# Attention with polynomial sketches and a squared-ReLU FFN on one core: five edits at the start, one at the end

## The chip, the core and the metric

The kernel runs on one NeuronCore of a Trainium2 chip. The metric is the device time of one execution in microseconds; before the change the median of three runs is 184.01 us (183.97 to 184.29). A profiled execution gives the trace from which the lines below come. The engines are TensorE (PE; its weight loads are PEld), VectorE (DVE), ScalarE (ACT), GpSimd (POOL), and SyncE (SP), which issues the DMAs.

## The reference

Batch 4, heads 4, sequence 1088, head dimension 32, sketch width 8, d_model 128, d_ff 2048:

```python
def phi(x):
    a = np.einsum('rd,bhsd->bhsr', S1, x)
    b = np.einsum('rd,bhsd->bhsr', S2, x)
    return np.einsum('bhsi,bhsj->bhsij', a, b).reshape(*x.shape[:-1], r * r)
q_p, k_p = phi(q), phi(k)
kv  = np.einsum('bhsf,bhsd->bhfd', k_p, v)
z   = np.sum(k_p, axis=2)
num = np.einsum('bhsf,bhfd->bhsd', q_p, kv)
den = np.einsum('bhsf,bhf->bhs', q_p, z)[..., None] + 1e-06
x   = (num / den) -> 4352 rows of 128        # heads side by side
out = np.maximum(x @ w_in, 0) ** 2 @ w_out
```

## The kernel before

**Stages.** Every query needs the sums `kv` and `z` of its whole batch, and every FFN row needs all four heads. The FFN is the bulk of the work: the 4352 rows are cut into ten chunks `FC` of 256 to 512 rows, and each chunk passes through 16 blocks of 128 hidden columns. One or two blocks together make a *unit*: `ffn1` (L600) multiplies by w_in into a PSUM tile `pg`, `relu` (L612, or L610 on VectorE) and `square` (L623 on ScalarE, L625 on VectorE) make `g`, and `ffn2` (L644) adds the block's share to the chunk's PSUM tile `po`. The second layer is in fp32 and takes two passes per matmul; the first is in fp32r and takes one. `f_oT` (L648) and `f_out` (L658) transpose and store a finished chunk; `f_last` (L666) stores the last one, whose two halves of 128 rows lie in two PSUM tiles, `po` and `pol`.

**The first 256 rows** are written out by hand (L702 to L857), for they stand before everything: k arrives and is transposed, `a_kf` (L313) multiplies four tiles of k by both sketches into PSUM tiles `kf`, ScalarE copies the second factor into `kb`, `a_kp0` (L331) multiplies the factors into `kp`, and `a_kv0` (L396) sums kp times v, and kp times ones, over nine tiles of 128 rows into the PSUM tile `kvp`. Meanwhile `q0` (L754) makes the queries' features. From `kvp` VectorE takes `zb`, `bd` and `zm`; then come the denominators `den0` (they begin with a matmul of `eps`, L790), the numerators `num0`, the reciprocals, and `xT`, the FFN's input.

**The chunks of attention after that** (batch 0 from row 256 on in two chunks, then each batch at a time) go through `q_tasks` and `nd_tasks`. `a_qc` sketches the queries on TensorE, `a_qt` to `a_rc` make the reciprocals of the denominators on VectorE (`rc`), `a_rl` (L508) places them by 16 small GpSimd copies into `rd`, `a_qs` and `a_qp` make the features, `a_nd` (L543) multiplies them by `kv` (64 small passes), `a_bc` (L559) spreads `rd` over the columns, and `a_x` multiplies into `xT`. The first of these chunks is called (0, 8): batch 0, rows 256 to 639.

**Order.** `tc.manual_schedule()` keeps every engine's instructions in the order in which they are written. Beyond the part by hand, `_Order` writes it: it plays the operations through with a cost for each engine, a key (a due time), the operations that each needs, and the number of buffers in each ring, and emits them by their planned start. The FFN's matmuls have a fixed sequence among themselves. An instruction waits by semaphores for what it really needs, and all that stands behind it on its engine waits too.

**PSUM rings.** `psf` has two tags, `pg` and `po`, of two tiles each, taken in turn. In the part by hand `pg` goes to a warm-up tile, `kf` of the second and fourth group, `kvp`, `num0`; `po` goes to `sp`, `kf` of the first and third group, `den0`, a warm-up tile. `kvp` takes the place of the second group's `kf`, and so waits until the second `kp` has read it.

**Loads.** All are issued by SP in one queue, and each waits until the one eight issues before it has landed. For batch 0: k, q's first 256 columns of each partition's row, v in eight pieces (L199), q's next 384; then the weights in quarters: w_in 0, 1, 2, w_o 0, 1, w_in 3, w_o 2, 3, then the rest of q. GpSimd casts each quarter of w_in to fp32r (`cast_wi`, L688) when it has landed. Quarter c serves the hidden blocks 4c to 4c + 3. Then the loads of batch 1 (k, four of v, q) and batch 2 stand in the queue.

Of the kernel before, what the change touches and what calls it, by code (L numbers as in the profile page):

```python
# [107 lines left out]
def kernel(  # L108
# [20 lines left out]
    LU = 4  # L129
    KC = [(0, 160), (160, 128)]  # L130
    W0, W1, W3 = 8, 0, 1
    ND, QT, WI, KL, QL = 2, 6.0, (1.0, 1.9), (30.0, 8.0), 4.0

# [24 lines left out]
    def sb(name, cols, dt=F32, rows=128):  # L160
        return cpool.tile([rows, cols], dt, tag=name, name=name)
# [80 lines left out]

    kt0 = sb("kt0", SP)
    nc.vector.memset(_ap(kt0, 0, 128, 128 * (NT - 2) + 96, [[128, 2], [1, 32]]), 0.0)
    eps = sb("eps", 192, rows=1)
    nc.vector.memset(eps[:, 0:64], 1e-6)
    nc.vector.memset(eps[:, 64:192], 1.0)
    zb = sb("zb", 130)
    nc.gpsimd.memset(zb[:, :], 0.0)
    own_p = sb("own_p", 2)  # L250
# [59 lines left out]
                )  # L310


    def a_kf(t0, n, pool, tag, w=32):  # L313
        kf = pool.tile([128, 512], F32, tag=tag, name="kf")
        for t in range(n):
            for c in range(0, 128, w):
                o = 128 * (t0 + t) + c
                nc.tensor.matmul(
                    _ap(kf, c, w, 32 * t, [[32 * n, 2], [1, 32]]),
                    kt0[:, o : o + w],  # L320
                    sf,
                )
        kb = wpool.tile([128, 32 * 3], F32, tag="kb", bufs=4, name="kb")
        nc.scalar.copy(kb[:, 0 : 32 * n], kf[:, 32 * n : 64 * n])
        st["kf", t0] = kf, kb
# [182 lines left out]
    def a_rl(b, i0, nb, c):  # L508
# [3 lines left out]
        for h in range(H):  # L512
# [2 lines left out]
                st["rc"][32 * c : 32 * c + 32, n * h : n * h + n],  # L515
            )

    def a_qs(b, i0, nb, which, x):
        m = 8 * nb
        if x == 0:  # L520
            st[b, which, i0] = wpool.tile([128, 4 * 32 * NT], F32, tag=which, bufs=1, name=which)
        nc.vector.stream_shuffle(  # L522
            in_=banks(st[b, "qc", i0], 2 * x, 0, m),
            out=_ap(st[b, which, i0], 0, 128, 2 * m * x, [[m, 2], [1, m]]),
            mask=mask_b if which == "qb" else mask_a[int(which[2])],
        )
# [139 lines left out]
    def f_last(c0):  # L666
        po, b = st["po", c0], B - 1


        def store(i):  # L670
            for x, eng in enumerate((nc.sync, nc.scalar)):
                eng.dma_start(
                    bass.AP(
                        out.tensor,
                        out.offset + (b * S + 16 * x * G + (c0 - b * S) // 32 + 4 * i) * 128,
                        [[G * 128, 16], [128, 4], [1, 128]],
                    ),
                    ob[i][64 * x : 64 * x + 64, :],
                )

        ob = [fpool.tile([128, 128], F32, tag="obl", bufs=2, name="obl") for _ in range(2)]
        nc.scalar.copy(ob[0][:, :], po[0][:, 0:128])
        store(0)
        nc.vector.tensor_copy(ob[1][:, :], po[1][:, 0:128])
        store(1)

    def cast_wi(c):
# [21 lines left out]
    nc.scalar.copy(ss[:, :], sp[:, 0:80])  # L709
    load_q(nc.sync, 0, 256, 640)  # L710
    load_wi(nc.sync, 0)
    load_wi(nc.sync, 1)
    load_wi(nc.sync, 2)
    load_wo(nc.sync, 0)
    load_wo(nc.sync, 1)
    load_wi(nc.sync, 3)
    for c in range(2, 4):
        load_wo(nc.sync, c)
    load_q(nc.sync, 0, 640, S)
    keep_warm(W1)  # L720
    keep_warm(1, 384)
    a_kT0(0, 2)
    a_kT0(2, 2)
    for x in range(2):
# [41 lines left out]
    a_kp0(0, 2)  # L766
    a_kf(2, 2, psf, "pg")
    a_kf(4, 3, psf, "po")
    a_kf(7, 2, psf, "pg", 64)
    q0(0)  # L770
    q0(1)
    for i in range(2):
# [1 line left out]
            _ap(qb0, 64 * i, 64, 0, [[256, 2], [1, 256]]),  # L774
            _ap(x0, 64 - 64 * i, 64, 0, [[512, 2], [1, 256]]),
        )
    st[0, "kvp"] = psf.tile([128, 512], F32, tag="pg", name="kvp")
    for t0, n in ((0, 2), (2, 2), (4, 3), (7, 2)):
        if t0:
            a_kp0(t0, n)  # L780
# [5 lines left out]
        in1=_ap(qb0, 0, 128, 0, [[256, 2], [1, 256]]), op=mult,  # L786
    )
    den0 = psf.tile([128, 512], F32, tag="po", name="den0")
    for y in range(2):
        nc.tensor.matmul(  # L790
            den0[64 * y : 64 * y + 64, 0:128], eps[0:1, 0:64], eps[0:1, 64:192],
            start=True, stop=False,
        )
    bd = sb("bd", 128)
    own = _ap(own_p, 0, 128, 0, [[0, 2], [1, 2], [0, 32]])

# [26 lines left out]
    for g in range(2):  # L823
        for y in range(2):
            o = 65 * y + 1 - g
            nc.tensor.matmul(  # L826
                den0[64 * y : 64 * y + 64, 0:128], zb[:, o : o + 64],
                qp0[:, 256 * y + 128 * g : 256 * y + 128 * g + 128], start=False, stop=(g == 1),
            )
    for y in range(2):  # L830
        nc.tensor.matmul(
# [56 lines left out]
    def q_tasks(b, i0, nb, key):  # L888
# [34 lines left out]
            ("rc", b, i0), {"DVE": 0.2 + 0.65 * more + nb * 17 / 960}, k0 - 0.1, [], on(a_rc, nb),  # L923
            uses=[("pd", b, i0)], rings=[("rc", 1)],
        )
        for c in range(4):
            O.add(
                ("rl", b, i0, c), {"POOL": 0.8 + 1.25 * more}, k0 + 0.1 * c, [], on(a_rl, b, i0, nb, c),
                uses=[("rc", b, i0)], rings=[("rd", 2)] if c == 0 else [],
            )  # L930
        for w_ in ("qb", "qa0", "qa1"):
# [15 lines left out]
    def nd_tasks(b, i0, nb, key):  # L947
        m = 16 * nb
        qps = [("qp", b, i0, e, x) for e in range(E) for x in range(2)]
        kb, vb = NK.get((b, i0)), NV.get((b, i0))  # L950

        O.add(
            ("nd", b, i0), {"PE": 0.6 + 1.05 * max(nb, 14) / 36}, key - 3.5 - 4 * dve(m),
            [("kvr", b, h) for h in range(H)]
            + ([("kT", kb, 0), ("kT", kb, 18)] if kb else [])
            + ([("vn", vb), ("ks", vb, 3)] if vb else []),
            on(a_nd, b, i0, nb, (0,) if kb or vb else (0, 1)), uses=qps + [("qp", b, i0, 0, 0)], rings=[("att", 1)], lag=PEL,
        )
        if kb:
            def behind(eng):  # L960
                a_kc(kb, st[b, "nd", i0], start=False)
                a_nd(b, i0, nb, (1,))

            glued(("kc", kb), 0.65, ("nd", b, i0), behind)
        if vb:
            def behind(eng):
                a_kvs(vb, st[b, "nd", i0], 32 * NT, start=False)
                a_nd(b, i0, nb, (1,))

            glued(  # L970
                ("kvs", vb), 1.25, ("nd", b, i0), behind, [("kp", vb, h) for h in range(H)],
            )
        for x in range(2):
            O.add(
                ("bc", b, i0, x), {"DVE": dve(m)}, key - 2.5 - 4 * dve(m) + 0.1 * x, [], on(a_bc, b, i0, nb, x),
                uses=[("rl", b, i0, 2 * x), ("rl", b, i0, 2 * x + 1)],
                rings=[("bc", 1)] if x == 0 else [],
            )
            O.add(
                ("x", b, i0, x), {"DVE": dve(m)}, key - 2.0 - 4 * dve(m) + 0.1 * x, [], on(a_x, b, i0, nb, x),  # L980
                uses=[("bc", b, i0, x), ("nd", b, i0)]
                + ([("kc", kb)] if kb else []) + ([("kvs", vb)] if vb else []),
            )

    def loads(b):
        load_k(nc.sync, b)
        for p in range(4):
            load_v(nc.sync, b, p)
        load_q(nc.sync, b, 0, S)

    prev["qTuse"] = []
    KB = {(0, 20): 1, (2, 0): 3}
# [2 lines left out]
    def k_load(b, k0, s0):  # L995
# [2 lines left out]
            [("kvs", b - 2), ("qc", b - 2, AC[b - 2][-1][0])] if b > 2 else [],  # L998
            on(loads, b), at=s0,
        )  # L1000
        for x, y, t in (("ld", "kn", 6.0), ("kn", "vn", 3.0), ("vn", "qn", 3.0)):
            O.add((y, b), {"IO": t}, s0, [(x, b)], lambda eng: None)
        for i0, n in ((0, 18), (18, 16)):
            O.add(
                ("kT", b, i0), {"DVE": dve(32 * n)}, k0, [("kn", b), ("kc", b - 1)],
# [166 lines left out]
```

## Time and profile before

| | |
|---|---|
| median of 3 runs | 184.01 us (183.97 to 184.29) |
| the profiled execution | 183.99 us, span 182.1 us |
| granted TensorE clock, mean | 0.998 |
| busy in the span | PE 177.3, ACT 136.6, DVE 122.1, PEld 104.6, POOL 39.1 us |
| largest groups | second FFN layer 122.7 us, first 70.2 us (their spans overlap), ReLU on ACT 75.3 us |
| first FFN matmul | at 12.17 us |
| first `po` matmul | at 13.89 us |
| last matmul ends | at about 178.9 us |

In the lines below, a timeline row gives start and duration in us, then engine, line, operation, the tiles `out<-in`, shapes and how many instructions the row holds; in square brackets stands the engine's idle time before it and what ended it. [...]

### The profile page before, as it was taken

How to read it: one execution, taken by the hardware profiler on the slowest of the kernel's cores; microseconds unless marked ns; L12 is line 12 of the kernel's file. 1: busy time of each engine (PE TensorE's matmuls, PEld its weight loads, DVE VectorE, ACT ScalarE, POOL GpSimd, SP SyncE). 2: the span in 40 equal slices, each digit the busy share in tenths (PEclk: the TensorE clock that was granted, in tenths of full speed). 3: DMA queues.
4: the chain of work that ended last, by engine and by line, in shares of the span. 5: the costliest groups of instructions: out<-in, count | busy, mean ns of one | idle time of the engine just before them, and what ended most of it. 6: DMA issues, size and time to landing. Idle time of an engine off the chain costs nothing.

```text
span 182.1 us, 3998 instructions
## 1 busy us (share of the span) xinstructions
PE 177.3 (97%) x1530; PEld 104.6 (57%) x1530; DVE 122.1 (67%) x262; ACT 136.6 (75%) x259; POOL 39.1 (21%) x158
## 2 busy tenths in 40 slices
PE   8999999999999999999999999999999999999992
PEld 2768776656555655655555554545554555555792
DVE  5979879999999951899994335996353334333640
ACT  3449679759947886799937778995777777777980
POOL 3545318348200003470018000600000000000000
PEclk9999999999999999999999999999999999999999
DMA  5799993010029700000031200003003000300211
GB/s 174 196 274 337 246 257 96 7 29 0 0 47 243 175 0 4 4 2 0 0 54 24 34 0 5 0 0 59 0 4 58 0 0 6 51 0 0 35 26 29
DMA packets 26146, 11.26 MB, mean 62 GB/s; under 512 B 17936, under 2 KB 25104, under 8 KB 26128
## 3 DMA queue, kind: packets, MB, share of 16 engines
q1 hardware_dynamic: 25936, 10.95, 24.8%
q8 instruction: 12, 0.20, 0.4%
q10 hardware_dynamic: 192, 0.07, 0.1%
q14 instruction: 6, 0.05, 0.1%
HBM read 8.78 MB, written 2.23 MB: 60 GB/s over the span
## 4 chain that ended last, share of the span: by engine, by line
PE 93%; DMA 2%; DVE 2%; SPq 0%; issue 0%; ACT 0%; ACTq 0%
PE po L644 61%; PE pg L600 18%; PE nd L553 3%; DMA qn<-in_q_dram 2%; PE po L639 2%; PE pol L639 2%; PE qc L306 1%; PE nd L417 1%; PE kvp L399 1%; PE qc L350 1%; PE kvp L417 1%; DVE kp L334 1%; SPq L181 0%; DVE g L625 0%; PE nd L350 0%; PE den L826 0%
## 5 line engine op out<-in xcount | busy, mean ns | idle before, releaser
L644 PE MATMUL po<-g,w_o 128*128 128x512 f32 (+3 forms) x288 | 122.7, 547 | 0.2 <-DVE g L625 0.2
L612 ACT ACTIVATE gt<-pg 128x512 f32<-128x512 f32 (+3 forms) x144 | 75.3, 570 | 31.4 <-PE pg L600 30.9
L644 PEld LDWEIGHTS po<-g,w_o 128*128 128x128 f32 x288 | 53.4, 189 | 32.3 <-issue 24.6
L600 PE MATMUL pg<-xT,w_in 128*128 128x512 f32 (+3 forms) x160 | 70.2, 520 | 0.0
L623 ACT ACTIVATE g<-gt 128x512 f32<-128x512 f32 (+2 forms) x102 | 60.7, 623 | 1.6
L625 DVE TENSOR_TENSOR g<-gt 128x512 f32<-128x512 f32 (+3 forms) x43 | 30.4, 708 | 39.5 <-ACT gt L612 38.8
L600 PEld LDWEIGHTS pg<-xT,w_in 128*128 128x128 f32 x160 | 29.2, 190 | 28.3 <-ACT gt L612 11.5
L513 POOL COPY rd<-rc 32x9 f32<-32x9 f32 (+2 forms) x80 | 19.6, 246 | 25.8 <-DVE rc L505 22.6
L459 POOL COPY kv<-kvt 32x64 f32<-32x64 f32 x48 | 12.7, 265 | 44.6 <-DVE kvt L436 42.5
L522 DVE STREAM_SHUFFLE qa<-qc 128x576 f32<-128x576 f32 (+2 forms) x20 | 11.8, 648 | 0.0
L537 DVE TENSOR_TENSOR qp<-qa,qb 128x576 f32<-128x576 f32 (+2 forms) x20 | 10.8, 604 | 0.0
L485 DVE STREAM_TRANSPOSE qt<-qc 128x576 f32<-128x576 f32 (+2 forms) x10 | 5.8, 608 | 6.2 <-PE qc L350 4.5
L370 DVE TENSOR_TENSOR kp<-fs 128x576 f32<-128x576 f32 x12 | 8.7, 741 | 0.0
L648 DVE STREAM_TRANSPOSE oT<-po 128x512 f32<-128x512 f32 (+3 forms) x9 | 5.9, 654 | 2.1 <-PE po L644 2.1
L553 PE MATMUL nd<-qp,kv 32*32 32x288 f32 (+2 forms) x320 | 6.6, 354 | 0.0
L522 DVE STREAM_SHUFFLE qb<-qc 128x576 f32<-128x576 f32 (+2 forms) x10 | 6.1, 651 | 0.0
L570 DVE TENSOR_TENSOR xT<-nd,bc 128x576 fp32r<-128x576 f32 (+2 forms) x10 | 5.6, 592 | 0.5 <-PE nd L553 0.5
L299 DVE STREAM_TRANSPOSE qT<-qn 128x192 f32<-128x192 f32 (+3 forms) x11 | 5.8, 554 | 0.2 <-DMA qn<-in_q_dram 0.2
L639 PE MATMUL po<-w_o,g 128*128 128x128 f32 x32 | 5.8, 280 | 0.0
L639 PE MATMUL pol<-w_o,g 128*128 128x128 f32 x32 | 5.7, 275 | 0.0
L563 DVE STREAM_TRANSPOSE bc<-rd 128x576 f32<-128x576 f32 (+2 forms) x10 | 5.7, 598 | 0.0
L553 PEld LDWEIGHTS nd<-qp,kv 32*32 32x32 f32 x320 | 2.9, 103 | 3.6 <-issue 2.4
(106 smaller groups left out, 89.2 us busy)
## 6 DMA issues: line engine op xcount, KB each, us to landing
kn<-in_k_dram SPq DMA_DIRECT2D x3, 544.0 KB, 7.2
qn<-in_q_dram SPq DMA_DIRECT2D x3, 544.0 KB, 7.8
vn<-in_v_dram SPq DMA_DIRECT2D x9, 144.0 KB, 6.0
w_in<-in_moe_w_in_dram SPq DMA_DIRECT2D x4, 256.0 KB, 4.2
w_o<-in_moe_w_out_dram SPq DMA_DIRECT2D x4, 256.0 KB, 5.1
out_dram<-oT SPq DMA_DIRECT2D x12, 64.0 KB, 1.9
out_dram<-oT SPq DMA_DIRECT2D x8, 56.0 KB, 1.9
out_dram<-oT SPq DMA_DIRECT2D x8, 48.0 KB, 1.8
```

The source lines that it names most:

```text
L370: nc.vector.tensor_tensor(out=_ap(st[b, "kp"], 0, 128, 64 * NT * h, [[64, NT], [8, 8], [1, 8]]), in0=_ap(fs, 0, 128, o, [[32, NT], [1, 8], ...
L459: nc.gpsimd.tensor_copy(_ap(st[b, "kv"], 32 * c, 32, 64 * h, [[32, E], [1, 32]]), _ap(st["kvt"], 32 * h, 32, 0, [[64, E], [1, 32]]),)
L513: nc.gpsimd.tensor_copy(st[b, "rd", i0][32 * h : 32 * h + 32, n * c : n * c + n], st["rc"][32 * c : 32 * c + 32, n * h : n * h + n],)
L522: nc.vector.stream_shuffle(in_=banks(st[b, "qc", i0], 2 * x, 0, m), out=_ap(st[b, which, i0], 0, 128, 2 * m * x, [[m, 2], [1, m]]), mask=m ...
L537: nc.vector.tensor_tensor(out=st[b, "qp", i0, e][:, r], in0=st[b, f"qa{e}", i0][:, r], in1=st[b, "qb", i0][:, r], op=mult,)
L553: nc.tensor.matmul(nd[32 * h : 32 * h + 32, 512 * c : 512 * c + m], kv[r, o : o + 32], qp[r, m * h : m * h + m], start=(e == 0), stop=(e = ...
L600: nc.tensor.matmul(st["pg", u][:, n * i : n * i + n], w_in[:, 128 * (d0 + i) : 128 * (d0 + i) + 128], xT[:, c0 : c0 + n],)
L612: nc.scalar.activation(gt[:, 0:w], st["pg", u][:, 0:w], Relu)
L623: nc.scalar.activation(to, of, Square)
L625: nc.vector.tensor_tensor(out=to, in0=of, in1=of, op=mult)
L639: nc.tensor.matmul(po[x // 128][:, 0:128], g[:, x : x + 128], w, start=(d == 0), stop=(d == NB - 1),)
L644: nc.tensor.matmul(po[0][:, 0:n], w, g, start=(d == 0), stop=(d == NB - 1))
```

## The change

1. *Reciprocals of chunk (0, 8).* The 16 GpSimd copies are replaced by one VectorE multiply (`a_rm`, masks `rc` into four column groups) and four TensorE matmuls (`a_rp`) with the replicated identity `irep`, which write the placed reciprocals into columns 384 to 395 of the first chunk's `po` bank; `a_bc` reads them there. In the order that results, the four stand between the two matmuls of unit 3 in `po`, and the two `bc` come directly behind the features, before a transpose of q; the other transpose of q goes behind the transposes of k. TensorE waits for the second `bc` before it goes on in `po` after `nd`. The other chunks keep the copies.
2. *The sums `kvp`* take a tile of the ring `po` in place of `pg`, hence the tile of the first group's `kf`. The fourth `kf` is made by eight matmuls of 32 columns as the others are, no longer four of 64. The `eps` matmul is one of 128 columns in place of two of 64. One warm-up matmul of 384 columns becomes three of 128.
3. *Loads.* The quarters come in the order w_in 0, w_o 0, w_in 1, w_in 2, w_o 1, w_in 3, w_o 2, then the rest of q, then w_o 3.
4. *v of batch 1* is held: a VectorE memset of one column of 32 partitions, in the order behind the last feature multiply of chunk (0, 8), writes into the tile, and the load has to wait for it. SP's queue waits with it: the rest of v and q of batch 1, the loads of batch 2, and the first stores. v's four pieces are loaded last one first, in every later batch too.
5. *The last copy* out of `pol` is halved: VectorE takes columns 0 to 63, ScalarE 64 to 127. In the program that results, ScalarE's half waits for VectorE's.

```diff
-    eps = sb("eps", 192, rows=1)
+    eps = sb("eps", 256, rows=1)
...
+    def a_rm(nb):
+        st["rx"] = wpool.tile([128, 4 * nb], F32, tag="rx", bufs=1, name="rx")
+        nc.vector.tensor_tensor(
+            out=_ap(st["rx"], 0, 128, 0, [[nb, 4], [1, nb]]),
+            in0=_ap(st["rc"], 0, 128, 0, [[0, 4], [1, nb]]),
+            in1=_ap(own_h, 0, 128, 0, [[1, 4], [0, nb]]), op=mult,
+        )
+
+    def a_rp(b, i0, nb):
+        st[b, "rd", i0] = st["po", 0][0][:, 384 : 384 + nb]
+        for h in range(H):
+            nc.tensor.matmul(
+                st["po", 0][0][32 * h : 32 * h + 32, 384 : 384 + nb],
+                irep[:, 0:32],
+                _ap(st["rx"], 0, 128, nb // 4 * h, [[nb, 4], [1, nb // 4]]),
+                start=False, stop=True, skip_group_check=True,
+            )
...
-        nc.vector.tensor_copy(ob[1][:, :], po[1][:, 0:128])
+        nc.vector.tensor_copy(ob[1][:, 0:64], po[1][:, 0:64])
+        nc.scalar.copy(ob[1][:, 64:128], po[1][:, 64:128])
...
     load_wi(nc.sync, 0)
+    load_wo(nc.sync, 0)
     load_wi(nc.sync, 1)
     load_wi(nc.sync, 2)
-    load_wo(nc.sync, 0)
     load_wo(nc.sync, 1)
     load_wi(nc.sync, 3)
-    for c in range(2, 4):
-        load_wo(nc.sync, c)
+    load_wo(nc.sync, 2)
     load_q(nc.sync, 0, 640, S)
+    load_wo(nc.sync, 3)
...
-    keep_warm(1, 384)
+    keep_warm(3, 128)
...
-    a_kf(7, 2, psf, "pg", 64)
+    a_kf(7, 2, psf, "pg")
...
-    st[0, "kvp"] = psf.tile([128, 512], F32, tag="pg", name="kvp")
+    st[0, "kvp"] = psf.tile([128, 512], F32, tag="po", name="kvp")
...
-    for y in range(2):
-        nc.tensor.matmul(
-            den0[64 * y : 64 * y + 64, 0:128], eps[0:1, 0:64], eps[0:1, 64:192],
-            start=True, stop=False,
-        )
+    nc.tensor.matmul(
+        den0[:, 0:128], eps[0:1, 0:128], eps[0:1, 128:256],
+        start=True, stop=False, skip_group_check=True,
+    )
...
+        if (b, i0) == (0, 8):
+            O.add(
+                ("rm", b, i0), {"DVE": 0.13}, k0 - 0.1, [], on(a_rm, nb), uses=[("rc", b, i0)],
+            )
+            O.add(
+                ("rp", b, i0), {"PE": 0.15}, -1000.0, [], on(a_rp, b, i0, nb),
+                uses=[("rm", b, i0)], lag=RL,
+            )
+        for c in range(4 if (b, i0) != (0, 8) else 0):
...
+    def loads_vq(b):
+        for p in range(3, -1, -1):
             load_v(nc.sync, b, p)
         load_q(nc.sync, b, 0, S)
+
+    def hold_v(b):
+        nc.vector.memset(_ap(vn[b], 96, 32, 32 * (NT - 2) - 1, [[32 * NT, H], [1, 1]]), 0.0)
...
+        if b == 1:
+            O.add(
+                ("hold", b), {"DVE": 0.07}, -500.0, [("qp", 0, 8, 1, 1)], on(hold_v, b),
+            )
+            O.add(("ldv", b), {"SP": 1.0}, s0, [("hold", b), ("ld", b)], on(loads_vq, b))
```

## The prediction

> **What bounds the kernel now.** I read the busy time by stretches first, then the chain that ended last, then the timeline around the three places that the diff touches on TensorE's path: the start of the FFN, the first attention chunk (rows 256 to 639 of batch 0), and the end.
>
> ```profile
> 13.90:170.00 156.10, 156.10 (x1215) 88.42 (x1216) 107.27 (x225) 123.34 (x235) 32.92 (x129) 1.00 0.21 50
> 178.90:182.10 3.20, 0.00 (x0) 0.00 (x0) 0.28 (x1) 0.00 (x0) 0.00 (x0) 0.91 0.15 41
> ...
> PE 93%; DMA 2%; DVE 2%; SPq 0%; issue 0%; ACT 0%; ACTq 0%
> ```
>
> Columns of the first two lines: stretch, length, then busy time of PE, PEld, DVE, ACT, POOL. From 13.9 to 170 us TensorE is busy 156.10 of 156.10 us, at a granted clock of 1.00, and the chain is TensorE for 93%. So three things alone move the time: when the first second-layer matmul (`po`) starts, what is put into or taken out of TensorE's queue after it, and the 3.2 us behind the last matmul. Work on VectorE, GpSimd or a DMA queue counts only if TensorE comes to wait for it.
>
> ```profile
> 12.65 0.42 DVE L610 TENSOR_SCALAR gt<-pg 128x256 f32<-128x256 f32 x1 [0.31 <-PE pg L600]
> 12.90 0.62 POOL L688 CAST w_in<-w_in 128x512 fp32r<-128x512 f32 x1 [0.97 <-DMA w_in<-in_moe_w_in_dram]
> 12.99 0.80 DVE L625 TENSOR_TENSOR g<-gt 128x256 f32<-128x256 f32 x1
> 13.22 0.47 PE L600 MATMUL pg<-xT,w_in 128*128 128x256 f32 x2
> 13.71 0.41 DVE L625 TENSOR_TENSOR g<-gt 128x256 f32<-128x256 f32 x1
> 13.89 0.45 PE L644 MATMUL po<-g,w_o 128*128 128x256 f32 x1 [0.19 <-DVE g L625]
> ```
>
> The start: `po` waits for the first square `g`, which takes 0.80 us where its twin takes 0.41. A GpSimd cast of a quarter of w_in runs from 12.90 to 13.52, and 13.52 + 0.27 (256 columns at VectorE's rate of the longer rows, about 0.96 per ns) is 13.79, where `g` ends: `g` stood still until the cast was done. TensorE itself was ready at about 13.53.
>
> ```profile
> 18.17 0.58 PE L600 MATMUL pg<-xT,w_in 128*128 128x256 f32 x2
> 18.69 0.96 PE L553 MATMUL nd<-qp,kv 32*32 32x96 f32 x64
> 19.58 1.99 PE L644 MATMUL po<-g,w_o 128*128 128x256 f32 x8
> ...
> 10.81 0.25 PE L836 MATMUL x<-zm,s2f 128*32 128x8 f32 x8
> ```
>
> What small matmuls between full-size ones cost. The steady spacing of passes is 0.216 us for 256 fp32 columns and 0.117 for fp32r, so the `pg` before `nd` streams until 18.60. The 64 passes of `nd` start between 18.69 and 19.41. The `po` after it starts to load weights at 19.58 and its second pass follows 0.32 later instead of 0.216, so it streams from 19.68. Of 1.08 us put in, 0.72 are passes and 0.36 are the two changes of tile shape: 0.09 in, 0.27 out.
>
> ```profile
> 177.99 0.27 ACT L682 COPY obl<-po 128x128 f32<-128x128 f32 x1 [0.80 <-PE po L639]
> 178.89 0.29 DVE L684 COPY obl<-pol 128x128 f32<-128x128 f32 x1 [2.20 <-PE pol L639]
> ...
> L324 ACT COPY kb<-kf x4: 213/213/240, 5.4 to 6.3; 128x64 f32<-128x64 f32 x3, 128x96 f32<-128x96 f32 x1
> ...
> ACT kvt L819 <- DVE zm L810: 1.9, 1, 1.9
> ```
>
> The end: after the last matmul one VectorE copy, then the store. The last line is from the list of waits: ScalarE's copy of `kvp` had to wait for VectorE's last read of the same PSUM tile, though it needs nothing from it; that hop took 0.09 us (9.99 to 10.08).
>
> **The change part by part**, against the profiled execution (183.99 us: span 182.1 and 1.89 around it; the median is 184.01).
>
> *Reciprocals through TensorE.* Taken away: 16 GpSimd copies (15.74 to 20.07, about 0.2 us each), for which one `bc` on VectorE waited until 20.10. No gain on the path: the second `xT` ended at 20.87, and its matmul could stream only at 21.41 (after eight `po` passes), some 0.4 us to spare. Added: one VectorE multiply 128x48, 0.19 us (`zm` 128x32 0.18, `pw` 128x64 0.20), and four matmuls, eight passes of 12 columns, set between the two `po` matmuls of unit 3. Nearest row: `x<-zm,s2f`, the same tile shape and count, whose passes start within 0.07 us. With both shape changes: 0.07 + 0.36 = 0.44 us (rounded from 0.073 + 0.365). All of it is on the path, since TensorE has no idle time there. Bounds: 0.07 (shape changes hidden) to 0.55 (if each pass took as long as the 0.02 of a `kf` pass and the weights came out worse). I take 0.44, since `nd` sits between the same neighbours. [...]
>
> *New waits by it.* `bc` now reads the `po` bank, so VectorE waits for the `po` matmuls of unit 4, and TensorE waits for the second `bc` before unit 5. VectorE's `qp` ended at 18.345; plus 0.19, up to 0.2 where the new multiply meets the cast at 15.18, the new 0.06 memset and two `bc` (0.30 apart, 0.37 long) gives 19.5; TensorE comes there at 19.58 + 0.44 = 20.02. Nothing, with 0.5 to spare. Then `qT`, `g`, two `xT`, two `kT` and the other `qT` (0.33, 0.57, 0.72, 1.37, 0.33) end at about 22.75 at the latest, and `qc` wants them at 22.71 + 0.44 = 23.15.
>
> *kv sums in the other ring, four `kf` 32 wide, one eps matmul.* The sums may start when the first `kp` (6.42) instead of the second (7.02) is done, so near 6.55 instead of 7.07. But their fifth tile waits for batch 0's last v load: it is issued at 5.45 and lands 2.5 us later, and there the passes, 58 ns apart, show their one gap (8.00 to 8.11). The 40 passes after it end as before, and `zb` with them. Nothing; if that gap were not v, up to 0.25. The 0.22 us saved in `kf` goes into a wait. The eps matmul ends before `zb` allows the next one: 0 to 0.05, taken as 0. Three 128-column warm matmuls against one of 384 are equal.
>
> *w_o's first quarter second.* The quarters of w_in now land first, third, fourth, sixth. `po`'s weights landed at 8.48 + 5.1 = 13.6, just in time; now earlier, which alone gives nothing. Against that, w_in's second quarter, cast at 11.31 before, lands where the third did: cast 12.90 to 13.52. The third `pg` unit (13.22 before) needs it, so its weights load from 13.61, and by the spacing of before (weights 13.19, end of stream 13.53) `po` can go at 13.95; before, its first pass really streamed from 13.96. `g` is held by the cast just as before. Sum: 0. Bounds: 0.36 earlier, if that quarter lands 0.4 earlier, to 0.4 later, if it lands as much later. The q columns moved ahead of w_o's last quarter, which unit 7 needs only after 21.5: nothing.
>
> *v of batch 1 held.* SP waits for a VectorE memset behind the last `qp` (about 18.7), and queued behind it are q of batch 1, k, v and q of batch 2 and the first stores. v issued at 14.2 to 16.5 had landed by 23.1 in the trace; 4.5 us later is 27.6, and it is needed at 34.53. k of batch 2 (27.1, needed at 38.94) and the first store (35.46) keep several us. Nothing; if that cover went, the sums of batch 1 would stop TensorE by what is late.
>
> *The last copy halved.* VectorE's half: 0.225 us (between 4 columns 0.165 and 128 columns 0.290). ScalarE's half waits for VectorE's in the changed program's order, as `kvt` did; 0.09 for the hop and 0.213 (`kb`, also 128x64). 0.225 + 0.09 + 0.213 - 0.290 = +0.24. Bounds: -0.07 (side by side) to +0.3.
>
> Sum: 0.44 + 0.24 + 0 = +0.68, so 184.67 in the profiled execution and 184.7 beside the median.
>
> **The rivals.**
> 1. *w_in's second quarter lands early* (not slower). If it lands by 12.45, its cast is over when `g` starts, and `po` goes at 13.53. Then -0.36 + 0.44 + 0.24 = +0.32, 184.3, within the noise of a comparison. For it: between 10 and 11.5 us, when quarters of w_in were moving, the DMA rate was near 200 to 250 GB/s, and 300 to 340 from 12 on with w_o among them, so a w_o quarter in second place may clear the way. Against: loads land in the order of their issue and as many bytes stand ahead.
> 2. *The cast moves onto VectorE's next squares.* The third quarter, landing at 13.6, is cast from 13.65, and the second `g` (13.71) is held like the first: +0.55 for VectorE, which eats the margins at `nd` and `qc`, and with a quarter landing 0.3 late the sum is 0.44 + 0.24 + 0.4 = +1.1, 185.1. It decides once VectorE is over 0.5 us behind. [...]
> 3. *The shape changes cost nothing and the halves run side by side*: 0.07 - 0.07 + 0, 184.0, no change; together with an early landing 183.6. Against it stand `nd` and `kvt`.
>
> **How the numbers follow.** Likeliest, chance 0.47: 184.7. Rival 1: 0.23, 184.3. Rival 2: 0.18, 184.9 to 185.1. Rival 3: 0.12, 183.6 to 184.0. The range 184.1 to 185.1 leaves out most of rival 3 and a little of rival 2; the likeliest alone spans 184.5 to 184.9. A comparison here can't tell less than 0.2% (0.37 us) from no change, so faster is below 183.64, slower above 184.38. Faster: part of rival 3 and what I overlook, 0.09. Same: two thirds of rival 1 and the rest of rival 3, with some of the likeliest's lower bounds, 0.26. Slower: 0.65.
>
> **What would show it.** The cast of the second quarter at about 12.9 and `po` at 13.9 to 14.0; four `po<-rx` matmuls with 0.4 us between the `po` passes around them beyond their spacing; no wait of TensorE at `nd`, unit 5 or `qc`; ScalarE's half starting after VectorE's and the last store issued about 0.5 us after the last matmul's result instead of 0.3. It is wrong if `po` starts by 13.6, if the passes around the new matmuls are under 0.2 us further apart than usual, or if TensorE stops between 18 and 24 us.

## The result, and the profile after

The changed kernel takes 185.61 us (median of six runs, 185.4 to 186.24) beside 184.15 us for the kernel before in the same comparison (six runs, 183.97 to 184.78): ratio 1.0079, 95% interval 1.0057 to 1.0101. It is slower by 1.46 us. In a later comparison (h3 below) it took 185.39 us beside 184.25, ratio 1.0056, interval 1.0033 to 1.0079. The prediction had 184.7 us and a range to 185.1: the side was right, the size about half of what came.

The profiled executions took 183.99 us (span 182.1) before and 185.51 us (span 183.4) after. The first view is the busy time by stretches of the changed kernel (stretch, length, then busy time of PE, PEld, DVE, ACT, POOL), then its chain and one group of its page.

```profile
13.90:170.00 156.10, 155.69 (x1221) 87.96 (x1221) 106.84 (x226) 122.49 (x234) 29.53 (x114) 1.00 0.22 51
```

```profile
PE 97%; issue 0%; ACT 0%; DVE 0%; ACTq 0%
...
L571 PE MATMUL nd<-qp,kv 32*32 32x288 f32 (+2 forms) x320 | 7.0, 354 | 0.4 <-issue 0.4
```

Before, TensorE was busy for all of the 156.10 us; now it lacks 0.41 us. The group line names the place: `nd`, once, idle 0.4 us, ended by "issue", which means that the engine waited for nothing that the profile shows: no semaphore, no DMA of the program, no other engine. The waits of the kernel before have no such line for `nd` on PE. The timeline shows where it is; the last line is the same row in the kernel before:

```profile
34.52 0.50 PE L571 MATMUL nd<-qp,kv 32*32 32x128 f32 x32
...
36.22 0.47 PE L571 MATMUL nd<-qp,kv 32*32 32x128 f32 x22
37.10 0.43 PE L571 MATMUL nd<-qp,kv 32*32 32x128 f32 x10 [0.41 <-issue]
...
35.80 0.50 PE L553 MATMUL nd<-qp,kv 32*32 32x128 f32 x32
```

This is the first chunk of batch 1: a row of 32 `nd` passes, 80 passes of kv sums, a second row of 32. The second row breaks after 22 passes; the 23rd starts 0.673 us after the 22nd (36.424 and 37.097), where neighbours are 0.007 apart. In the kernel before, the row's first and last pass start 0.234 us apart (35.802, 36.036), after the change 1.033: 0.80 us, with some slower steps right behind the stop (the longest 0.077 us).

The start, the new matmuls and the end, from the timeline of the changed kernel:

```profile
12.18 0.62 POOL L707 CAST w_in<-w_in 128x512 fp32r<-128x512 f32 x1 [1.20 <-DMA w_in<-in_moe_w_in_dram]
...
13.23 1.16 DVE L643 TENSOR_TENSOR g<-gt 128x256 f32<-128x256 f32 x2
13.38 0.74 POOL L707 CAST w_in<-w_in 128x512 fp32r<-128x512 f32 x1 [0.58 <-DMA w_in<-in_moe_w_in_dram]
...
13.77 0.65 PE L662 MATMUL po<-g,w_o 128*128 128x256 f32 x2
```

```profile
16.43 0.59 PE L662 MATMUL po<-g,w_o 128*128 128x256 f32 x2
...
16.96 0.25 PE L529 MATMUL po<-rx,irep 128*32 128x12 f32 x8
```

```profile
180.04 0.22 DVE L702 COPY obl<-pol 128x64 f32<-128x64 f32 x1 [2.22 <-PE pol L657]
180.30 0.21 ACT L703 COPY obl<-pol 128x64 f32<-128x64 f32 x1 [0.88 <-DVE obl L702]
180.54 0.56 ACTq L690 DMA_DIRECT2D out_dram<-obl  x1
```

At the start, the cast of w_in's second quarter ran at 12.18 instead of the predicted 12.90 and was over before the first `g` (13.235 to 13.647, 0.41 us); but the next cast, 13.38 to 14.12, stood across the second `g` (13.567 to 14.396, 0.83 us). Around the four `rx` matmuls, from the `po` pass at 16.43 to the first `nd` pass, it is 2.670 us; between the same passes before, 2.290. At the end, ScalarE's half starts 0.034 us after the end of VectorE's, and from the last matmul pass to the store's issue it is 0.81 us instead of 0.63.

Where the 1.52 us between the two profiled executions come from, by the start times of the same passes in both traces. Starts are compared and not ends, since the rows of neighbours overlap: in the kernel before, a `po` pass of 256 columns lasts 0.38 us in its row, and the next one starts 0.216 us behind it.

| stretch | us |
|---|---|
| start, up to `po` of unit 2 (16.397, 16.432) | +0.04 |
| the `rx` matmuls (`po` of unit 4: 17.497, 17.909) | +0.38 |
| from there to the first `nd` of batch 1 (34.101, 34.523) | +0.01 |
| the broken row of `nd`, up to the next `po` (36.233, 37.454) | +0.80 |
| behind it, up to 60 us (59.327, 60.356) | -0.19 |
| 119 us of equal work up to the last pass (178.574, 179.727) | +0.12 |
| last pass to the store's issue | +0.18 |
| the store's issue to the end of the span (2.93, 2.89) | -0.04 |
| outside the span (1.85, 2.08) | +0.23 |

The +0.12 is 2.183 to 2.184 us for a unit of 512 rows instead of 2.180; e3, f5, g3 and h3 below, which have both `rp` and the stop described next, have it too; e1, with `rp` and no stop, and e2, with the stop and no `rp`, do not. No run settles why. What lies outside the span differs between executions: 1.77 to 2.35 us in the runs below, without order. The -0.19 is time made up behind the delay. From the `po` pass behind 41.6 us to the one behind 59.3 us it is 17.68 us in the kernel before and 17.53 in every run below that had lost time at 36 to 40 us, most of it at two passes near 55.4 and 55.9 us that the kernel before starts late; what they wait for is not shown.

### The profile page after: what moved, and what is told of

It is laid out like the page before. It is cut to its first block, busy times and chain, and to the rows that moved or that the text cites. A ratio compares the mean times of both kernels' runs of the same rounds, so it can differ in the third digit from the quotient of the medians.

```text
span 183.4 us, 4018 instructions
## 1 busy us (share of the span) xinstructions
PE 178.5 (97%) x1546; PEld 105.3 (57%) x1546; DVE 122.5 (67%) x264; ACT 136.8 (75%) x260; POOL 35.6 (19%) x142
## 4 chain that ended last, share of the span: by engine, by line
PE 97%; issue 0%; ACT 0%; DVE 0%; ACTq 0%
PE po L662 61%; PE pg L618 18%; PE nd L571 4%; PE warm L714 2%; PE po L657 2%; PE pol L657 2%; PE qc L306 2%; PE nd L417 1%; PE kvp L399 1%; PE kf L318 1%; PE qc L350 1%; PE kvp L417 1%; PE nd L350 0%; PE x L776 0%; PE den L844 0%
## 5 line engine op out<-in xcount | busy, mean ns | idle before, releaser
L513 POOL COPY rd<-rc 32x9 f32<-32x9 f32 (+1 forms) x64 | 15.9, 249 | 29.8 <-DVE rc L505 27.2
L581 DVE STREAM_TRANSPOSE bc<-rd 128x576 f32<-128x576 f32 (+1 forms) x8 | 4.9, 656 | 0.0
```

What stands on the lines that cost most here:

```text
L513: nc.gpsimd.tensor_copy(st[b, "rd", i0][32 * h : 32 * h + 32, n * c : n * c + n], st["rc"][32 * c : 32 * c + 32, n * h : n * h + n],)
```

## What stopped TensorE

My first theory, A: a block of TensorE's own instructions had not arrived. Besides the loads, the page of each kernel has a line for DMAs of kind "instruction" (here the changed kernel's; the kernel before has the same with 0.4%):

```profile
q8 instruction: 12, 0.20, 0.5%
```

That is twelve packets of 16 KB in a span. I counted TensorE's instructions in the order of the program, two for each pass (weights and matmul) and one for each wait of its own: 3103 before, 3135 after, 259 and 261 to a packet. The change adds 32 up to the stop: `rp` 16, the fourth `kf` in eight matmuls instead of four 16, two more warm-up matmuls 4, and one eps matmul less takes 4. The stop stands exactly ahead of the 1217th; 256 before it is the 961st, the eighth pass of the first `nd` row, and it is there that the trace has a packet. The DMA view of that stretch holds this one packet and nothing else:

```profile
DMA packets 1, 0.02 MB, mean 11 GB/s; under 512 B 0, under 2 KB 0, under 8 KB 0
...
q8 instruction: 1, 0.02, 5.2%
```

The window is 34.4 to 35.9 us; the packet starts at 34.566 and takes 1.24 us. Between the two borders lie small passes alone, which TensorE gets through in 1.86 us (34.569 to 36.43); the first instruction of the next block started 2.53 us after the packet. In the kernel before, the later border lay on a long `po` pass, 3.7 us behind the earlier one.

Rival B: the stop belongs to the place, to an operand, a bank or an engine that `nd` waits for. Then shifting the stream without touching anything there would leave it.

### The stream shifted, in both directions

```diff
-    keep_warm(W0)
+    keep_warm(24, 170)
```

The eight opening filler matmuls of 512 columns become 24 of 170: nearly the same columns, 32 more instructions. The same edit went into the changed kernel (e1) and into the kernel before (e2).

> The changed kernel with its eight opening filler matmuls of 512 columns cut into 24 of 170: the same columns in the same time, 32 TensorE instructions more ahead of everything else. Theory A (instruction blocks): the changed kernel stops for 0.67 us in the middle of a row of nd matmuls (36.424 to 37.097 us) because TensorE's instruction stream enters a new block of 256 instructions there, 2.5 us after it entered the one before, and the block has not come. 32 instructions more move both borders forward in the program, the earlier one back into the long matmuls ahead of nd, so that some 4 us lie between them: no stop, and 185.6 - 0.8 = 184.8 us. Theory B (the stop belongs to the place: an operand, a bank or another engine that nd waits for): the stop stays at the same matmul, 185.6 us.

> The kernel before with the same 24 fillers of 170 columns in place of 8 of 512, nothing else. Its TensorE stream is then as long up to nd as the changed kernel's. Theory A (instruction blocks): the same stop appears in the same row of nd matmuls of batch 1, within some four matmuls of the place that it has in the changed kernel, 0.6 to 0.8 us, and the time is 184.15 + 0.7 to 0.8 = 184.9 us. Theory B: nothing that nd waits for has changed, no stop, 184.15 us.

e1: 184.72 us beside 184.33, ratio 1.0029 (1.0007 to 1.0052). e2: 185.32 us, ratio 1.0058 (1.0033 to 1.0083). Timeline of the second row in e1:

```profile
36.62 0.50 PE L571 MATMUL nd<-qp,kv 32*32 32x128 f32 x32
```

The same row in e2, the kernel before with smaller fillers:

```profile
36.47 0.47 PE L553 MATMUL nd<-qp,kv 32*32 32x128 f32 x22
37.40 0.43 PE L553 MATMUL nd<-qp,kv 32*32 32x128 f32 x10 [0.46 <-issue]
```

In e1 the stop is gone. Both borders lie 16 passes earlier: the first among long matmuls, where the packet started at 31.32, and the second behind the sixth pass of this row, 5.3 us after that packet. So here, with the packet early, the border crossed in this row costs nothing by itself (two runs with an idle time left open stand further below). In e2 the kernel before, in which nothing else was altered, has got the stop, at the same 22nd pass, 0.73 us. Rival B has fallen. e2 was some 0.4 us slower than expected; its trace shows an added wait at the start, which comes back below.

### A smaller shift

```diff
-    keep_warm(W0)
+    keep_warm(16, 256)
```

> The changed kernel with 16 opening fillers of 256 columns in place of 8 of 512: 16 TensorE instructions more, half of what took the stop away. Theory A (instruction blocks): the earlier border now falls on the last po pass ahead of nd, about 0.45 us before its place in the changed kernel (34.11 against 34.57 us), the later one eight nd passes sooner. A block that takes 2.5 us from border to first use (34.569 to 37.097 us in the changed kernel) then leaves a stop of 0.2 to 0.4 us, eight passes earlier in the row; none if the sequencer reads ahead of the long passes. Against the run with 32 more instructions (no stop) 0 to 0.4 us. Theory C (any shift of the stream takes the stop away, whatever its size): no stop.

```profile
36.21 0.44 PE L571 MATMUL nd<-qp,kv 32*32 32x128 f32 x14
37.08 0.46 PE L571 MATMUL nd<-qp,kv 32*32 32x128 f32 x18 [0.43 <-issue]
```

185.33 us, ratio 1.0052 (1.0019 to 1.0084). The stop moved by the eight passes expected, so theory C has fallen, but it kept its size (0.70 us) instead of shrinking. By the count the earlier border is on the last `po` pass (34.096), as expected; but the packet did not start there, only at 34.446, beside the first `nd` pass (34.511). From the packet's start to the first instruction of the block it took 2.64 us. In the six runs with a stop this time is 2.53, 2.54, 2.30, 2.64, 2.37 and 2.58 us (after, e2, e3, f5, g3, h3). So the stop lasts until 2.3 to 2.6 us behind the packet's start. The packet itself was over before TensorE came to the border in all six (in the changed kernel at 35.81, the border at 36.43), and the first instruction followed 1.27 to 1.49 us after the packet's end. What fills that time no run shows; by theory A the block was not yet usable, though its packet had ended.

In the changed kernel TensorE gets through 256 instructions in 1.86 us between the two borders, against 2.3 to 2.6 us from a packet's start to the first instruction of its block; in the kernel before it takes 3.7 us between the borders, and there is no stop.

## The parts one by one

### `rp` alone, in the kernel before

```diff
-        for c in range(4):
...
+        if (b, i0) == (0, 8):
+            O.add(
+                ("rm", b, i0), {"DVE": 0.13}, k0 - 0.1, [], on(a_rm, nb), uses=[("rc", b, i0)],
+            )
+            O.add(
+                ("rp", b, i0), {"PE": 0.15}, -1000.0, [], on(a_rp, b, i0, nb),
+                uses=[("rm", b, i0)], lag=RL,
+            )
+        for c in range(4 if (b, i0) != (0, 8) else 0):
```

The functions `a_rm` and `a_rp` and the wait of `bc` for `rp` come with it, as in the change.

> The kernel before with rp alone: the reciprocals of units 2 and 3's neighbours (the group behind the first eight) go through rx and four TensorE matmuls instead of GpSimd's copies; loads, kv sums, den and last copy as before. It adds 16 instructions to TensorE's stream. Theory A (instruction blocks): rp costs 0.38 us where it stands, and its 16 instructions pull the later border of the pair from the po pass behind the nd rows of batch 1 to the thirtieth of the 32 passes of the second row, 1.9 us behind the row's start; the block comes 2.3 to 2.6 us after its packet starts, so the stop is 0.5 us at least, just ahead of the row's last two passes: 184.2 + 0.4 + 0.5 or more = 185.1 to 186. Theory B (no part of the stop is rp's): 184.2 + 0.4 = 184.6 us, no stop.

```profile
16.25 0.59 PE L662 MATMUL po<-g,w_o 128*128 128x256 f32 x2
16.78 0.25 PE L529 MATMUL po<-rx,irep 128*32 128x12 f32 x8
...
18.92 0.96 PE L571 MATMUL nd<-qp,kv 32*32 32x96 f32 x64
```

```profile
36.05 0.49 PE L571 MATMUL nd<-qp,kv 32*32 32x128 f32 x30
37.35 0.37 PE L571 MATMUL nd<-qp,kv 32*32 32x128 f32 x2 [0.81 <-issue]
```

185.52 us beside 184.22, ratio 1.0070 (1.0043 to 1.0096). From 16.254 to 18.924 it is 2.670 us, so `rp` costs 0.38 us where it stands, as in the changed kernel. And its 16 instructions alone bring the stop, ahead of the last two passes as counted beforehand. The stop is 1.07 us long, longer than in the changed kernel: the packet started only at 34.987, 0.54 us behind the earlier border (34.451). This one part gives about as much loss as the whole change, in part by a longer stop. The fourth `kf` in eight matmuls also adds 16 instructions and by the count would put the border at the same place; that was not run.

### `rp` taken out of the changed kernel

```diff
-    keep_warm(W0)
+    keep_warm(32, 128)
...
-            O.add(
-                ("rp", b, i0), {"PE": 0.15}, -1000.0, [], on(a_rp, b, i0, nb),
-                uses=[("rm", b, i0)], lag=RL,
-            )
-        for c in range(4 if (b, i0) != (0, 8) else 0):
...
+        for c in range(4):
...
-                uses=[("rl", b, i0, 2 * x), ("rl", b, i0, 2 * x + 1), ("rp", b, i0)],
+                uses=[("rl", b, i0, 2 * x), ("rl", b, i0, 2 * x + 1)],
```

> The changed kernel with the reciprocals of the units behind the first eight moved by GpSimd's copies again, as before the change (no rx, no rp), and 32 fillers of 128 columns at the start, which put the borders of the instruction blocks where they are in the run with 24 fillers. Theory: rp costs its 0.38 us on TensorE's chain and nothing hides behind it: that run's time less 0.38, so about 184.4 us, and po of unit 4 starts 0.38 us sooner against xT's end. Rival: with v held and GpSimd's copies behind a later start, bc comes too late for unit 5 and TensorE waits there: 184.8 us or more.

```profile
16.43 1.03 PE L662 MATMUL po<-g,w_o 128*128 128x256 f32 x4
...
18.72 0.96 PE L571 MATMUL nd<-qp,kv 32*32 32x96 f32 x64
```

The same stretch is 2.291 us now (16.430 to 18.721): the 0.38 us are back, and there is no stop. The second `xT`, which waits for GpSimd's copies, ends at 21.268, and the first-layer matmul behind it comes 0.16 us later than the spacing would have it; so the rival's wait exists, and it is smaller than `rp`. The profiled execution took 184.25 us, near the 184.4 expected, but the median is 185.23, ratio 1.0052 (1.0029 to 1.0075): a miss that the part itself does not explain. See the fillers below.

### The last copy

```diff
-        nc.vector.tensor_copy(ob[1][:, 0:64], po[1][:, 0:64])
-        nc.scalar.copy(ob[1][:, 64:128], po[1][:, 64:128])
+        nc.vector.tensor_copy(ob[1][:, :], po[1][:, 0:128])
```

e3 is the changed kernel with this edit; f4 is the kernel before with the reverse of it.

> The changed kernel with its last output copy whole on VectorE again. If the two halves run one behind the other (0.223 and 0.212 us with 0.034 between in the changed kernel's trace, against 0.290 for the whole), the time from the last matmul pass to the store's issue goes from 0.81 back to 0.63 us and the kernel takes 185.6 - 0.2 = 185.4 us. If the end is set by something else (the store of the other half), 185.6 us. The stop in nd is there in either case.

> The kernel before with its last output copy in two halves, VectorE and then ScalarE, and nothing else. By the traces so far the halves run one behind the other: 0.63 us from last pass to the store's issue become 0.81, so 184.3 + 0.2 = 184.5 us. If the halves ran side by side, 184.25 us.

```profile
179.15 0.23 DVE L684 COPY obl<-pol 128x64 f32<-128x64 f32 x1 [2.20 <-PE pol L639]
179.41 0.21 ACT L685 COPY obl<-pol 128x64 f32<-128x64 f32 x1 [0.89 <-DVE obl L684]
179.65 0.56 ACTq L672 DMA_DIRECT2D out_dram<-obl  x1
```

The lines are f4's. From the last pass to the store's issue: 0.63 us in e3 and 0.81 in f4, each the reverse of its base. Medians: e3 185.49 (ratio 1.0059, 1.0039 to 1.0078), f4 184.42 beside 184.20 (1.0020, 0.9999 to 1.0042). The halves cost 0.18 us at the end of the trace; the medians cannot settle so little. The stop in `nd` is there in e3, 0.52 us.

### The loads

```diff
     load_wi(nc.sync, 0)
+    load_wo(nc.sync, 0)
     load_wi(nc.sync, 1)
     load_wi(nc.sync, 2)
-    load_wo(nc.sync, 0)
...
+    load_wo(nc.sync, 2)
     load_q(nc.sync, 0, 640, S)
+    load_wo(nc.sync, 3)
```

f1 is the kernel before with the new order; g4 the kernel before with v of batch 1 held; g2 has both.

> The kernel before with the order of the weights' loads of the changed one and nothing else: w_o's first quarter second, queries ahead of w_o's last. Theory: w_o's quarter is there by 11.3 us, its gate value comes before the cast of w_in's quarter 1 instead of behind it, so that po starts 0.2 to 0.4 us sooner after the first pg pass, of which the second gate value, held by the next cast, gives back 0.1 to 0.2: 0 to 0.2 us faster, 184.1 to 184.3 beside before at 184.3. Rival: the gain is lost in later quarters and it is the same from unit 2 on. No stop in nd in either case.

> The kernel before with v of batch 1 held by VectorE's zero and nothing else. Theory: k of batch 1 lands about 1 us earlier, v of batch 1 later, neither ends a wait of TensorE: the same, 184.2 us, and kT of batch 1 is done 0.5 to 1 us sooner. Rival: v of batch 1, behind the hold, ends a wait of the kv sums at 34.5 us: 184.4 us or more. No stop in nd.

> The kernel before with the changed order of the weights' loads and the held v of batch 1 together. With the order alone po started 0.34 us sooner after the first pg pass and lost it again by 25 us, where k of batch 1 landed 1 us later than in before and qc of unit 6 waited for kT. Theory: the hold brings that landing back below 21 us, the gain after the losses of the second gate value (0.1 to 0.2 us) stays: 184.05 us beside 184.2. Rival: the second gate value eats it all: 184.2 us. No stop in nd.

f1: 184.37 us beside 184.20, ratio 1.0007 (0.9989 to 1.0026). g4: 184.19 beside 184.22, 1.0007 (0.9980 to 1.0034). g2: 184.45 beside 184.22, 1.0026 (1.0000 to 1.0052). None is faster. In f1 `po` started 1.38 us after the first `pg` instead of 1.72, and `nd` came 6.32 us after it instead of 6.51. My expectation for g2 took this for a gain by the new order, but it is none: f4, g3 and g4, which keep the old order, have 1.37 as well, and f4 and g4 6.32. In these the cast that held the first `g` in the profile of the kernel before (12.90) ran at 12.53, 12.30 and 12.00 and was over in time. In g4:

```profile
12.00 0.62 POOL L688 CAST w_in<-w_in 128x512 fp32r<-128x512 f32 x1 [0.24 <-DMA w_in<-in_moe_w_in_dram]
...
13.04 0.75 DVE L625 TENSOR_TENSOR g<-gt 128x256 f32<-128x256 f32 x2
...
13.58 0.65 PE L644 MATMUL po<-g,w_o 128*128 128x256 f32 x2
```

So the held `g` of the kernel before belongs to that one execution, and not to its order of loads.

Behind `nd`, f1 lost time: GpSimd's copies came later (the second `bc` at 20.50 instead of 20.10), the second `xT` ended at 21.27 instead of 20.87, and the first-layer matmul behind it left 0.20 us later than in the kernel before (21.419 and 21.222). My expectation for g2 laid this loss on k of batch 1, which landed at 21.79 instead of 20.84; f1's trace shows no wait of TensorE for it. Only in f2, in the next section, did k land later still (22.21) and stop TensorE. With the hold alone k landed at 19.66 as expected, in g2 at 21.11, not below 21 as expected, and nothing waited for it. In g2's profiled execution the quarters landed so that `po` started at 14.3.

### Without the three costs

> The kernel before with three parts of the change: the order of the weights' loads, the kv sums in the po ring, and one eps matmul of 128 columns in place of two of 64; GpSimd's reciprocals, the loads of batch 1 and the whole last copy stay. Theory (rp, the halved copy and the stop in nd are what made the change slow): no slower than before, 0 to 0.3 us faster, 184.0 to 184.3 us. Rival (the kv sums' place or the eps matmul delays the start, where the changed kernel's xT ended 0.24 us later): 184.5 us.

> The changed kernel without its three costs: the reciprocals by GpSimd's copies, the last copy whole, and 32 opening fillers of 128 columns that keep the borders of the instruction blocks out of the nd rows of batch 1; the loads, the kv sums in the po ring, the held v and the eps matmul of the change stay. Theory: from the first pg pass to the third nd row as with GpSimd's reciprocals and fillers (21.78 us, before: 21.93), and 0.63 us from last pass to the store's issue: 184.0 to 184.2 us, no slower than before. Rival (a cost that is none of the three): 184.5 us or more.

f2 (the kernel before with the new order of loads, kv sums in the `po` ring, and one eps matmul): 184.46 beside 184.20, 1.0020 (1.0000 to 1.0039). From the row of `qc` at 22.520 to `po` at 25.614 it lost 0.64 us on the kernel before, since k landed at 22.21 and kT came late; the view of the tile kT has this line among those that waited for it:

```profile
PEld qc L350: 0.8, 2
```

That is the rival's side, by another mechanism, and with an interval that begins at no change.

g1 (the changed kernel with GpSimd's copies, a whole last copy, 32 fillers of 128 columns): 184.83 beside 184.22, 1.0045 (1.0016 to 1.0073), again its rival's side. But g1's list of waits for TensorE at the start has a line that the first profiles of the kernel before and of the changed kernel lack:

```profile
PE kvp L399 <- DMA vn<-in_v_dram: 1.0, 1, 1.0
```

e2, which has fillers too, has the same line with 0.8. More instructions at the opening bring the stream's first border forward in the program. In these two the first block's packet started at 6.65 and 6.63 us instead of 8.01 in the kernel before, in the middle of v's loads, and v's last piece landed at 8.81 and 8.84 us instead of 7.97. Theory D says that this costs g1 its time; rival E, that a kept part of the change does. The last runs tell them apart: h2 has the same parts as g1 without added fillers (its opening is that of the kernel before), h3 is the changed kernel again.

```diff
-    keep_warm(32, 128)
+    keep_warm(W0)
...
-    keep_warm(3, 128)
+    keep_warm(1, 384)
...
-    a_kf(7, 2, psf, "pg")
+    a_kf(7, 2, psf, "pg", 64)
```

> The run without the three costs again (order of the weights' loads, kv sums in the po ring, held v, one eps matmul; GpSimd's reciprocals, whole last copy), now with no fillers at the start: the opening is the kernel before's (8 fillers of 512 and one of 384, the last kf 64 wide), and by count the second border of the instruction blocks falls on the qc row behind the nd rows of batch 1 without help. Theory D (the fillers cost at the start: they bring the first border forward, the 16 KB of the first block travel at 6.65 us instead of 7.8, and v's last piece lands at 8.8 instead of 7.6 us where the clock was high early): 184.0 to 184.3 us, no stop, first block behind 7.2 us, first pg pass near 12.2 us. Rival E (a cost in the parts kept): 184.7 us or more again, as with the fillers.

> The changed kernel once more, beside the same runs of before. Theory (its loss is rp, the stop and the halved copy): 185.5 us, a stop of 0.5 to 0.8 us at the same pass of the second nd row. The opening settles one thing more: if its TensorE clock rises at some other time than 6.1 us in this execution, the slow opening of the changed kernel's profile belongs to the execution and not to the change.

h2: 184.34 beside 184.25, ratio 1.0003 (0.9987 to 1.0019), no stop in `nd`, first packet at 8.00 us, v's last piece at 7.55, no wait for v. The first `pg`, though, came at 12.68 instead of 12.2, behind an opening that was late (its sums began at 7.65 us instead of 7.07); that this belongs to the execution is argued from the last section, not shown. E has fallen: the order of loads, the ring, the hold and the eps matmul together show neither cost nor gain. What is left for g1's time is its opening with the fillers: `xT` ended at 12.95 us in g1, at 12.58 in h2. That the early packet delayed v is argued from two runs: in g2 a packet started at 7.01 and v landed at 7.53. For e4, whose profiled execution had no such wait, that the fillers made its median slow is argued, not shown. h3: 185.39, ratio 1.0056, a stop of 0.66 us at the same pass. It has no added fillers and yet waits 0.4 us for v, which landed at 8.08, for its sums began early, at 6.69; so that wait alone is no sign of fillers.

Open: in f2 and h2 the border of the later block falls on the row of `qc` behind 39 us, and TensorE idles 0.2 to 0.3 us there with "issue" as the reason, though the packet had started over 3.5 us before. No run settles why.

No run points to a version that beats the kernel before: the one without the three costs and without fillers is level with it.

## Why the prediction was right or wrong

- *`rp`, +0.44 from 0.07 of passes and 0.36 of tile changes.* Right in kind, all of it on the path; 0.38 measured, in the changed kernel and in g3: 0.07 of passes as said, so 0.31 for the tile changes. The 0.4 us to spare that it gave GpSimd's copies were gone in e4 and f1, where the matmul behind them came 0.16 and 0.20 us late.
- *New waits by `rp`, 0 with 0.5 to spare.* In the profiled execution the second `bc` ended at 19.66 and `po` of unit 5 started at 19.99, without a wait. In e3 and h3 TensorE stood idle there for 0.09 and 0.13 us until just behind the second `bc`; the margin was smaller than thought.
- *The last copy, +0.24.* ScalarE's half did wait. 0.18 measured: the term that was off is the hop, taken as 0.09 from `kvt`'s row, 0.034 here.
- *Start of `po`, 0.* The sum came out (+0.04 at unit 2) by luck. The changed kernel's profile had a late opening, the first `pg` at 12.41 us instead of 12.17, which belongs to that execution (last section). From there to unit 2 it took 4.02 us instead of 4.22: the quarter landed at 12.13, rival 1's event, and `po` started 1.36 us behind `pg` instead of 1.72; then the next cast held the second `g`, rival 2's event. The prediction priced the two apart, and they came together. Nor is the 4.22 the kernel before's: f4, g3 and g4 with the old order have 4.02 to 4.03, so the held `g` that the prediction started from was one execution's.
- *kv ring, eps matmul, hold, order of loads, each 0.* No cost or gain shows in h2, which has the four together, nor in g4, the hold alone. What was said of the ring is seen in h3: the sums began sooner and then waited for v's last piece. The fourth `kf` in eight matmuls stands in no run alone; its 16 instructions belong to the shift that the next point is about.
- *The step that failed* is the sum's premise that what is "put into or taken out of TensorE's queue" costs the time of its passes, its changes of tile shape and the waits for other engines, and nothing else; it had no term for the instructions themselves. TensorE needs its instructions too, here twelve packets of 16 KB in a span, with borders 256 instructions apart by the count that e1, e2, f5 and g3 bore out, and 32 more of them moved a border into a dense stretch of short passes at batch 1: +0.80, of which 0.19 came back. The only threat that the prediction saw to batch 1 was a late v; v was in time.
- *The signs to look for.* It named a stop between 18 and 24 us; the stop came at 36.4, twelve us behind that window and 19 us behind the new matmuls.

With the stop, the prediction's own terms come to 0.04 + 0.38 + 0.18 + 0.80 - 0.19 = 1.21 us of the 1.52; the rest is the 0.12, the 0.23, the -0.04 and the 0.01 of the table.

## What to carry to other kernels

Count the bound engine's instructions, not only their time: where some hundred short ones follow one another (here 256 within 1.86 us), an edit far ahead (here 19 us) can put a border of the instruction stream into them, and the profile then shows idle time released by "issue" in a row that nobody touched. Before blaming or praising such an edit, shift the stream with a few fillers and see whether the idle time moves by as many instructions; and watch what the fillers themselves do to the start: here g1 with them was slower than h2 without. A single median then judges the shift, not the idea: here the part whose 16 instructions bring the stop also costs 0.38 us by its passes, and only the trace separates the two. The start teaches a second thing: a wait read from one profile, such as the held `g`, may belong to that execution; here more profiles with the same order of loads showed it.

## What the runs showed of the hardware

Besides the instruction blocks, the rate of the opening's passes. In some executions TensorE's small `kf` passes start at about half the rate, in the changed kernel's profile four of them every 0.107 us instead of every 0.056, and the moment of the change differs from execution to execution. Passes in the stretch from 5 to 6 us (the first count in each line), for the kernel before, the changed kernel, f4 (the opening of the kernel before) and h3 (the changed kernel again):

```profile
5.00:6.00 1.00, 1.00 (x62) 0.91 (x62) 0.76 (x3) 0.48 (x3) 0.88 (x5) 1.00 0.79 164
5.00:6.00 1.00, 1.00 (x37) 0.87 (x38) 0.47 (x2) 0.21 (x2) 0.82 (x4) 1.00 0.88 187
5.00:6.00 1.00, 1.00 (x36) 0.87 (x39) 0.43 (x2) 0.21 (x2) 0.82 (x4) 1.00 0.77 182
5.00:6.00 1.00, 1.00 (x72) 0.98 (x72) 0.74 (x3) 0.44 (x3) 0.88 (x5) 1.00 0.71 196
```

So the slow opening of the changed kernel's profile, 0.24 us at xT's end, belongs to the execution: the kernel before has it in f4, the changed kernel lacks it in h3. The granted clock, the last figure but two, stands at 1.00 in all four lines; but the records of the clock in these traces begin only at 4.06, 6.15, 6.40 and 4.15 us, and in the two late ones the passes speed up right there (6.18 and 6.41). So the spacing of the passes is what to read. In one execution of the changed kernel the spacing of four `kf` passes changes from 0.107 to 0.056 us at 6.18 us, in the other before 5.02 us. What sets the moment no run shows.
